# Retention and a wave MLP on one core: the first batch loaded with two tokens per partition in 512-byte rows, and computed by pairs of chunks on 64 by 64 tiles of the array

## The chip, the cores and the metric

The kernel runs on one core of one Trainium2 chip. The metric is the device time in microseconds (us), lower is better. Each run also gives the span from the first to the last instruction and the mean granted clock of TensorE over that span, 1.0 being full speed. A run is called slow here when it is more than 1.5% above the fastest run of the same kernel; ratios use fast runs alone.

## The reference, cut to what matters

```python
# q, k, v: [4 batches, 8 heads, 768 tokens, 64], float32
for t in range(S):                                  # retention, per batch and head
    state = gamma * state + outer(k[t], v[t])
    y[t] = scale * q[t] @ state
x = y with heads side by side                       # [4, 768, 512]
theta = x @ w_theta                                 # 512 x 512
y = w_tok_r @ (x * cos(theta)) + w_tok_i @ (x * sin(theta))   # over tokens, 768 x 768
u = x + y
out = u + relu(u @ w_ch)                            # 512 x 512
```

The kernel cuts the 768 tokens of a batch into six chunks of 128. Within a chunk the recurrence is a masked product of scores (k by q, then by v), and a running state of 64 by 64 a head carries what came before. A token position in a chunk is one of the 128 partitions.

## The kernel before

The loads of the weights and of the first 13 chunks are issued at the start, in an order chosen by hand, on SP's queue; those of the later chunks follow slot by slot. Of q, k and v a chunk is loaded with one token on each partition; a head gives each partition 64 floats, so each row of the transfer is 256 bytes.

```python
def load_chunk(n):
    b, c = divmod(n, nT)
    for name, src in (("kf", k), ("qf", q), ("vf", v)):
        t = io.tile([P, H, D], FT, name=name, bufs=9)
        nc.sync.dma_start(out=t, in_=src[b, :, c*P:(c+1)*P, :].rearrange("h s d -> s h d"))
for what in ("c0 c1 th c2 c3 c4 w0 c5 w1 w2 c6 w3 ch c7 c8 w4 c9 c10 w5 c11 c12").split(): ...
```

"c" is a chunk (three tensors of 256 KB), "th" and "ch" are w_theta and w_ch (1 MB each), "w" a block of 128 rows of each of w_tok_r and w_tok_i (384 KB each; called a pair of w_tok rows below). GpSimd scales and casts a chunk (att_prep), TensorE (PE) transposes k and q (att_T), DVE copies that out (kqT), PE makes the scores (att_A), DVE multiplies by the mask (at), PE makes the products and the state (att_Y), ACT copies the result and the state out, and att_X projects to the angles, of which ACT takes sines and DVE makes z (att_Z). The first batch runs as a software pipeline: chunk n begins while chunk n-1 is finished.

```python
att_prep(0)
for n in range(nT):
    att_T(n)
    if n > 0:
        att_Yinter(n - 1); att_Y(n - 1)
    att_A(n)
    if n > 0: att_X(n - 1)
    if n > 1: att_Z(n - 2)
    ...                                   # w_cast, w_tok, moe_M of the first outputs (cut)
    if n + 1 < nT: att_prep(n + 1)
```

After the first batch a second loop of slots interleaves the attention of chunks 6 to 23 with the products of w_tok by z (moe_M), of u by w_ch (moe_O), and the transposes of w_tok (w_tok). w_ch is cast by GpSimd in slot 0 of that loop.

## Time and profile before

| what | value |
|---|---|
| time, median of the first 3 runs | 184.55 us (183.6 to 186.36) |
| the profiled run | 185.79 us, span 184.0, clock 0.979 |
| PE busy | 161.1 us of 184.0 |
| end of the first batch's part on PE | 42.2 us |
| from there to the end | 141.8 us |

"The first batch's part" ends on PE when three things are done: the third pair of w_tok rows and chunk 6 are transposed, and the products of the first two outputs are complete. I call the time up to that point the head, and the time after it the tail. Two views that the prediction does not show: the stretch from the first to the sixth score group (stretch, length; then busy time and count of PE, PEld, DVE, ACT, POOL; clock, DMA share, GB/s), and from the timeline of PE the end of the head and two later waits (start, duration, engine, line, operation; in brackets the idle time before it and what ended it).

```profile
7.95:31.98 24.03, 19.42 (x207) 12.38 (x208) 14.50 (x19) 12.08 (x23) 15.84 (x17) 1.00 1.18 256
```

### The profile page before, as it was taken

To read this page: it belongs to the slowest core of one execution; us is meant where nothing else is said; L and a number is where in the kernel's file an instruction comes from. 1 tells how busy PE (TensorE), PEld (TensorE's weight loads), DVE (VectorE), ACT (ScalarE), POOL (GpSimd) and SP (SyncE) were. 2 spreads that over 40 slices of the span, in tenths; PEclk is the share of its full clock that TensorE was granted. 3 is DMA by queue.
4 is the path that set the end of the run, shared out by engine and by line. 5 is a ranking of instruction groups with operands and counts; after the bars stand their busy time and mean duration, and the time that the engine had idled before them with its cause. 6 is when DMAs were issued, how large, how long until landed. Compare 5 with 4: busy or idle time off the path is not lost.

```text
span 184.0 us, 3550 instructions
## 1 busy us (share of the span) xinstructions
PE 161.1 (88%) x1392; PEld 91.6 (50%) x1392; DVE 106.1 (58%) x146; ACT 72.6 (39%) x136; POOL 79.9 (43%) x105
## 2 busy tenths in 40 slices
PE   0567997795499989799999999999999999999991
PEld 0244655452265656555655565555545544444560
DVE  1264684736155877868976686756556634534442
ACT  4052754640044645554734544265354342200010
POOL 4648767691977669655859455231000000000000
PEclk9999999999579999999999999999999999999998
DMA  6999999998999989999999999954483333334343
GB/s 133 222 316 218 227 254 279 284 286 242 229 279 218 288 177 222 257 277 231 242 210 254 260 224 188 203 143 114 110 108 100 101 85 77 107 118 114 111 122 116
DMA packets 95265, 35.63 MB, mean 194 GB/s; under 512 B 89488, under 2 KB 89744, under 8 KB 95248
## 3 DMA queue, kind: packets, MB, share of 16 engines
q1 hardware_dynamic: 95104, 35.27, 85.4%
q8 instruction: 11, 0.18, 0.5%
q10 hardware_dynamic: 144, 0.13, 0.2%
q14 instruction: 6, 0.05, 0.1%
HBM read 25.69 MB, written 6.29 MB: 174 GB/s over the span
## 4 chain that ended last, share of the span: by engine, by line
PE 63%; SPq 15%; DMA 9%; DVE 5%; POOL 3%; ACT 1%; issue 1%; DVEq 0%; POOLq 0%
PE y_ps L282 29%; SPq L80 12%; PE o_ps L310 10%; PE th_ps L253 8%; DMA w<-in_moe_w_ch_dram 5%; DMA wtok<-in_moe_w_tok_r_dram 3%; PE at_ps L185 3%; PE yT_ps L214 3%; PE kq_ps L165 3%; SPq L94 2%; PE st_ps L222 2%; DVE at L189 2%; PE x_ps L250 2%; PE yT_ps L203 2%; DMA uT<-u 2%; DVE z L264 1%
## 5 line engine op out<-in xcount | busy, mean ns | idle before, releaser
L282 PE MATMUL y_ps<-z,wtr 128*128 128x512 bf16 x138 | 53.1, 385 | 1.5 <-DVE z L264 1.0
L282 PE MATMUL y_ps<-z,wti 128*128 128x512 bf16 x138 | 53.1, 385 | 0.0
L189 DVE TENSOR_TENSOR at<-at_ps,mask 128x1024 bf16<-128x1024 f32 x24 | 29.3, 1220 | 9.4 <-PE at_ps L185 9.4
L258 ACT ACTIVATE cs<-th_ps,halfpi 128x512 bf16<-128x512 f32 x24 | 16.5, 687 | 38.5 <-PE th_ps L253 38.5
L264 DVE TENSOR_TENSOR z<-cs,x_sb 128x1024 bf16<-128x1024 bf16 x24 | 20.8, 865 | 15.1 <-ACT cs L259 15.0
L154 POOL TENSOR_TENSOR kqb<-qf,qsc 128x512 bf16<-128x512 f32 x24 | 25.2, 1052 | 8.9 <-DMA qf<-in_q_dram 8.7
L156 POOL TENSOR_TENSOR vb<-vf,vsc 128x512 bf16<-128x512 f32 x24 | 25.4, 1060 | 7.5 <-PE yT_ps L214 3.3
L253 PE MATMUL th_ps<-wth,xT 128*128 128x512 bf16 x96 | 25.5, 389 | 1.9 <-DVE wth L393 1.9
L168 DVE COPY kqT<-kq_ps 128x1024 bf16<-128x1024 bf16 x19 | 13.1, 689 | 21.0 <-PE kq_ps L165 21.0
L153 POOL CAST kqb<-kf 128x512 bf16<-128x512 f32 x24 | 16.4, 684 | 18.8 <-DMA kf<-in_k_dram 8.1
L165 PE MATMUL kq_ps<-ident,kqb 128*128 128x128 bf16 x152 | 13.9, 238 | 11.7 <-POOL kqb L153 8.8
L287 DVE TENSOR_TENSOR u<-y_ps,x_sb 128x512 bf16<-128x512 f32 x23 | 15.8, 689 | 13.7 <-PE y_ps L282 13.7
L310 PE MATMUL o_ps<-wch,uT 128*128 128x512 bf16 x92 | 23.5, 380 | 0.1
L231 ACT CAST xT<-yT_ps 128x512 bf16<-128x512 f32 x24 | 14.0, 585 | 24.1 <-PE yT_ps L214 24.0
L313 DVE SCALAR_TENSOR_TENSOR ot<-o_ps,u 128x512 f32<-128x512 f32 x23 | 15.8, 690 | 10.2 <-PE o_ps L310 10.1
L282 PEld LDWEIGHTS <-wti 128*128 128x128 bf16 x138 | 13.6, 99 | 15.5 <-issue 2.6
L282 PEld LDWEIGHTS <-wtr 128*128 128x128 bf16 x138 | 13.6, 99 | 14.1 <-DVE wtr L334 0.7
L165 PEld LDWEIGHTS <-kqb 128*128 128x128 bf16 x152 | 11.0, 106 | 16.8 <-POOL kqb L153 9.2
L259 ACT ACTIVATE cs<-th_ps,zerob 128x512 bf16<-128x512 f32 x24 | 16.3, 680 | 0.0
L236 ACT CAST stbd<-st_ps 64x256 bf16<-64x256 f32 x40 | 14.7, 366 | 0.5
L295 ACT COPY uT<-u_ps 128x512 bf16<-128x512 bf16 x12 | 7.0, 585 | 18.5 <-PE u_ps L293 18.5
L310 PEld LDWEIGHTS <-uT 128*128 128x128 bf16 x92 | 8.7, 98 | 9.8 <-DMA uT<-u 0.3
(51 smaller groups left out, 149.0 us busy)
## 6 DMA issues: line engine op xcount, KB each, us to landing
kf<-in_k_dram SPq DMA_DIRECT2D x24, 256.0 KB, 4.8
qf<-in_q_dram SPq DMA_DIRECT2D x24, 256.0 KB, 5.1
vf<-in_v_dram SPq DMA_DIRECT2D x24, 256.0 KB, 5.3
out_dram<-ot SPq DMA_DIRECT2D x23, 256.0 KB, 2.2
wtok<-in_moe_w_tok_r_dram SPq DMA_DIRECT2D x6, 384.0 KB, 5.3
wtok<-in_moe_w_tok_i_dram SPq DMA_DIRECT2D x6, 384.0 KB, 5.1
w<-in_moe_w_theta_dram SPq DMA_DIRECT2D x1, 1024.0 KB, 6.7
w<-in_moe_w_ch_dram SPq DMA_DIRECT2D x1, 1024.0 KB, 8.5
```

Of the source, the lines that this page charges most:

```text
L80: nc.sync.dma_start(out=t, in_=src[b, :, c * P:(c + 1) * P, :].rearrange("h s d -> s h d"))
L153: nc.gpsimd.tensor_copy(kb.rearrange(r3, h=H), raw[n, "kf"])
L154: nc.gpsimd.tensor_mul(qb.rearrange(r3, h=H), raw[n, "qf"], _bcast_last(qsc[:, c], D))
L156: nc.gpsimd.tensor_mul(vb.rearrange(r3, h=H), raw[n, "vf"], _bcast_last(vsc[:, c], D))
L165: nc.tensor.transpose(kq_ps[:, i * NP + j, :], src[:, j * P:(j + 1) * P], ident)
L189: nc.vector.tensor_mul(at.rearrange("p a j t -> p (a j) t"), at_ps.rearrange("p a j t -> p (a j) t"), _bcast_mid(mask, H))
L253: nc.tensor.matmul(th_ps, s["xT"][:, j, :], wth[:, j, :], start=(j == 0), stop=(j == NP - 1))
L258: nc.scalar.activation(cs[:, 0, :], th_ps, AF.Sin, bias=halfpi, scale=1.0)
L259: nc.scalar.activation(cs[:, 1, :], th_ps, AF.Sin, bias=zerob, scale=1.0)
L264: nc.vector.tensor_mul(zs[b][:, c], st[n]["cs"], _bcast_mid(xs[b][:, c, :], 2))
L282: nc.tensor.matmul(y_ps, wT[r][:, s0, t0 * P:(t0 + 1) * P], zs[b][:, s0, r, :], start=(s0 == 0 and r == 0), stop=(s0 == nT - 1 and r == 1))
L310: nc.tensor.matmul(o_ps, mo[m]["uT"][:, j, :], wch[:, j, :], start=(j == 0), stop=(j == nD - 1))
```

## The change

The intent is to load the first batch in rows twice as long, hoping for a higher DMA rate while the kernel starts. Two neighbouring tokens are adjacent in memory, so a partition that takes both gets 512 bytes in one row. A pair of chunks (256 tokens) is then one tile of 128 partitions by two tokens, and a chunk of 128 tokens is 64 partitions by two. So the scores of a pair become products of 64 by 64, on four tiles of the array. The core of the diff:

```diff
+    def load_pair(g):
+        for name, src in (("k", k), ("q", q), ("v", v)):
+            t = io.tile([P, H, 2 * D], FT, name="pair", bufs=5)
+            nc.sync.dma_start(out=t, in_=src[0, :, 2*g*P:2*(g+1)*P, :].rearrange(
+                "h (p two) d -> p h (two d)", two=2))
...
-    "c0 c1 th c2 c3 c4 w0 c5 w1 w2 c6 w3 ch c7 c8 w4 c9 c10 w5 c11 c12"
+    loads("p0 th p1 w0 p2 w1 w2 c6 w3 c7 ch c8 w4 c9 c10 w5 c11 c12")
...
+    def pair_A(g, two):
+        at_ps = psum.tile([P, 2, NP, P], FT, name="at_ps", tag="at", bufs=1)
+        for j in range(NP):
+            for a in range(2):
+                half = slice(a * HP, (a + 1) * HP)
+                for par in range(2):
+                    rows = slice(par * D, (par + 1) * D)
+                    nc.tensor.matmul(at_ps[half, par, j, :], kT[rows, j, two, half],
+                                     qT[rows, j, :, half], ...)
+        nc.vector.tensor_mul(at..., at_ps..., maskp...)
...
-    for n in range(nT):            # the pipelined loop shown above
+    def pair_in(g):
+        pair_prep(g, "k"); pair_T(g, "k"); pair_prep(g, "q")
+        if g > 0: att_Z(2 * g - 1)
+        pair_T(g, "q"); pair_prep(g, "v")
+        pair_A(g, 0); pair_A(g, 1); pair_Y(g)
+    pair_in(0)
+    att_X(0); att_X(1); att_Z(0)
+    pair_in(1)
+    w_cast(0); att_X(2); w_tok(0); att_X(3); moe_M(0, 0, 2); att_Z(2)
+    pair_in(2)
+    moe_M(0, 2, 4); w_cast(1); att_X(4); w_tok(1); att_X(5); ...
...
-            nc.gpsimd.tensor_copy(wch, wdma["ch"])      # slot 0
+            wch_cast(0, nD)                             # slot 2, four casts on ACT
```

Cut: the second set of decay factors and the mask for pairs, pair_T, pair_Y, fewer buffers for the chunks that are left (7 instead of 9, and 1 instead of 2 for w_theta and w_ch), and the products with w_ch a slot later. In the order of loads chunk 7 also moves ahead of w_ch.

More of the change, by code (lines that the diff above doesn't have):

```diff
@@ L54 @@
     P = 128
+    HP = P // 2
     nT = S // P
@@ L78, in load_chunk @@
         for name, src in (("kf", k), ("qf", q), ("vf", v)):
-            t = io.tile([P, H, D], FT, name=name, bufs=9)
+            t = io.tile([P, H, D], FT, name=name, bufs=7)
             nc.sync.dma_start(
@@ L82, in load_chunk @@
             raw[n, name] = t
+    def load_pair(g):
+        for name, src in (("k", k), ("q", q), ("v", v)):
+            t = io.tile([P, H, 2 * D], FT, name="pair", bufs=5)
+            nc.sync.dma_start(out=t, in_=src[0, :, 2 * g * P:2 * (g + 1) * P, :].rearrange(
+                "h (p two) d -> p h (two d)", two=2))
+            raw[g, name] = t
     wdma = {}
     def load_w512(name, src):
-        t = io.tile([P, nD, dm], FT, name="w512", bufs=2)
+        t = io.tile([P, nD, dm], FT, name="w512", bufs=1)
         nc.sync.dma_start(out=t, in_=src.rearrange("(a p) e -> p a e", p=P))
@@ L95, in load_wtok, with loads @@
         wdma[r, t0] = t
-    for what in ("c0 c1 th c2 c3 c4 w0 c5 w1 w2 c6 w3 ch c7 c8 w4 c9 c10 w5 c11 "
-                 "c12").split():
-        if what == "th":
-            load_w512("th", moe_w_theta)
-        elif what == "ch":
-            load_w512("ch", moe_w_ch)
-        elif what[0] == "c":
-            load_chunk(int(what[1:]))
-        else:
-            for r in range(2):
-                load_wtok(r, int(what[1:]))
+    def loads(order):
+        for what in order.split():
+            if what == "th":
+                load_w512("th", moe_w_theta)
+            elif what == "ch":
+                load_w512("ch", moe_w_ch)
+            elif what[0] == "w":
+                for r in range(2):
+                    load_wtok(r, int(what[1:]))
+            elif what[0] == "p":
+                load_pair(int(what[1:]))
+            else:
+                load_chunk(int(what[1:]))
+    loads("p0 th p1 w0 p2 w1 w2 c6 w3 c7 ch c8 w4 c9 c10 w5 c11 c12")
     posn = const.tile([P, nT], FT)
@@ L127 @@
     nc.scalar.activation(qsc, arg, AF.Exp, bias=lscale, scale=1.0)
+    posp = const.tile([P, nT], FT)
+    nc.gpsimd.iota(posp, pattern=[[2 * P, nT // 2], [1, 2]], base=1,
+                   channel_multiplier=2, allow_small_or_imprecise_dtypes=True)
+    argp = const.tile([P, nT, H], FT)
+    nc.vector.tensor_mul(argp, _bcast_last(posp, H), _bcast_mid(lg, nT))
+    vscp = const.tile([P, nT, H], FT)
+    nc.scalar.activation(vscp, argp, AF.Exp, bias=zerob, scale=-1.0)
+    qscp = const.tile([P, nT, H], FT)
+    nc.scalar.activation(qscp, argp, AF.Exp, bias=lscale, scale=1.0)
     ident = const.tile([P, P], BF)
@@ L133 @@
                             base=0, pattern=[[1, P]], channel_multiplier=-1)
+    maskp = const.tile([P, 2, 2, HP], BF)
+    nc.gpsimd.memset(maskp, 1.0)
+    for a in range(2):
+        for two in range(2):
+            part = maskp[a * HP:(a + 1) * HP, two]
+            nc.gpsimd.affine_select(out=part, in_=part, compare_op=ALU.is_ge, fill=0.0,
+                                    base=-two, pattern=[[1, 2], [2, HP]],
+                                    channel_multiplier=-2)
     stbd = []
@@ L168, in att_T @@
         nc.vector.tensor_copy(kqT, kq_ps)
-        s["kqT"] = kqT
+        s["kT"], s["qT"] = kqT[:, 0:NP, :], kqT[:, NP:2 * NP, :]
     def att_T_dma(n):
@@ L175, in att_T_dma, with pair_prep @@
             out=kqT, in_=s["kqb"].rearrange("p a d -> p (a d)"))
-        s["kqT"] = kqT
+        s["kT"], s["qT"] = kqT[:, 0:NP, :], kqT[:, NP:2 * NP, :]
+    def pair_prep(g, name):
+        t = work.tile([P, 2, dm], BF, name="kqb", bufs=5)
+        src = raw[g, name].rearrange("p h (two d) -> p two h d", two=2)
+        dst = t.rearrange("p two (h d) -> p two h d", h=H)
+        if name == "k":
+            nc.gpsimd.tensor_copy(dst, src)
+        else:
+            for two in range(2):
+                sc = (qscp if name == "q" else vscp)[:, 2 * g + two]
+                nc.gpsimd.tensor_mul(dst[:, two], src[:, two], _bcast_last(sc, D))
+        st[g, name] = t
@@ new lines, in pair_T @@
+    def pair_T(g, name):
+        ps = psum.tile([P, NP, 2, P], BF, name="kq_ps", tag="tr", bufs=2)
+        for two in range(2):
+            for j in range(NP):
+                nc.tensor.transpose(ps[:, j, two, :],
+                                    st[g, name][:, two, j * P:(j + 1) * P], ident)
+        t = work.tile([P, NP, 2, P], BF, name="kqT", bufs=4)
+        nc.vector.tensor_copy(t, ps)
+        st[g, name + "T"] = t
+    def pair_A(g, two):
+        at_ps = psum.tile([P, 2, NP, P], FT, name="at_ps", tag="at", bufs=1)
+        kT, qT = st[g, "kT"], st[g, "qT"]
+        for j in range(NP):
+            for a in range(2):
+                half = slice(a * HP, (a + 1) * HP)
+                for par in range(2):
+                    rows = slice(par * D, (par + 1) * D)
+                    nc.tensor.matmul(at_ps[half, par, j, :], kT[rows, j, two, half],
+                                     qT[rows, j, :, half], start=(j == 0),
+                                     stop=(j == NP - 1), skip_group_check=True)
+        at = work.tile([P, 2, NP, P], BF, name="at", bufs=2)
+        nc.vector.tensor_mul(at.rearrange("p a j t -> p (a j) t"),
+                             at_ps.rearrange("p a j t -> p (a j) t"),
+                             _bcast_mid(maskp[:, two].rearrange("p w i -> p (w i)"), H))
+        st[g, two] = at
@@ new lines, in pair_Y @@
+    def pair_Y(g):
+        yT = [psum.tile([P, NP, P], FT, name="yT_ps", tag="acc", bufs=2)
+              for _ in range(2)]
+        for two in range(2):
+            at, vp = st[g, two], st[g, "v"]
+            for j in range(NP):
+                for a in range(2):
+                    half = slice(a * HP, (a + 1) * HP)
+                    for par in range(2):
+                        h = 2 * j + par
+                        nc.tensor.matmul(yT[a][par * D:(par + 1) * D, j, :],
+                                         vp[half, two, h * D:(h + 1) * D],
+                                         at[half, par, j, :],
+                                         start=(two == 0 and j == 0),
+                                         stop=(g == 0 and a == 0 and two == 1
+                                               and j == NP - 1),
+                                         skip_group_check=True)
+        for a in range(2):
+            c = 2 * g + a
+            half = slice(a * HP, (a + 1) * HP)
+            if c > 0:
+                for j in range(NP):
+                    nc.tensor.matmul(yT[a][:, j, :], stbd[c % 2][:, j, :],
+                                     st[g, "qT"][:, j, :, half], start=False,
+                                     stop=(j == NP - 1), skip_group_check=True)
+            if c < nT - 1:
+                if c == 0:
+                    st_ps[0] = psum.tile([P, NP, P], FT, name="st_ps", tag="st", bufs=1)
+                for two in range(2):
+                    for j in range(NP):
+                        nc.tensor.matmul(st_ps[0][:, j, :],
+                                         st[g, "k"][half, two, j * P:(j + 1) * P],
+                                         st[g, "v"][half, two, j * P:(j + 1) * P],
+                                         start=(c == 0 and two == 0 and j == 0),
+                                         stop=(c == nT - 2 and two == 1 and j == NP - 1),
+                                         skip_group_check=True)
+                state_out(0, c)
+            if c == 0:
+                x_tiles(0)
+            xT = work.tile([P, NP, P], BF, name="xT", bufs=3)
+            nc.scalar.copy(xT.rearrange("e j (i w) -> e j w i", w=2),
+                           yT[a].rearrange("e j (w i) -> e j w i", w=2))
+            st[c] = dict(xT=xT)
@@ L178, in att_A, with state_out, x_tiles @@
+    def state_out(b, c):
+        for par in range(2):
+            sl = slice(par * D, (par + 1) * D)
+            nc.scalar.copy(stbd[(c + 1) % 2][sl, :, sl], st_ps[b][sl, :, sl])
+    def x_tiles(b):
+        xs[b] = big.tile([P, nT, dm], BF, name="x_sb")
+        zs[b] = big.tile([P, nT, 2, dm], BF, name="z")
     def att_A(n):
         s = st[n]
-        kqT = s["kqT"]
         at_ps = psum.tile([P, 2, NP, P], FT, name="at_ps", tag="at", bufs=1)
@@ L184, in att_A @@
                 rows = slice(par * D, (par + 1) * D)
-                nc.tensor.matmul(at_ps[:, par, j, :], kqT[rows, j, :],
-                                 kqT[rows, NP + j, :], start=(j == 0),
+                nc.tensor.matmul(at_ps[:, par, j, :], s["kT"][rows, j, :],
+                                 s["qT"][rows, j, :], start=(j == 0),
                                  stop=(j == NP - 1), skip_group_check=True)
@@ L203, in att_Yinter @@
                 nc.tensor.matmul(s["yT_ps"][:, j, :], stbd[c % 2][:, j, :],
-                                 s["kqT"][:, NP + j, :], start=(j == 0), stop=False,
+                                 s["qT"][:, j, :], start=(j == 0), stop=False,
                                  skip_group_check=True)
@@ L227, in att_Y @@
         if c == 0:
-            xs[b] = big.tile([P, nT, dm], BF, name="x_sb")
-            zs[b] = big.tile([P, nT, 2, dm], BF, name="z")
+            x_tiles(b)
         xT = work.tile([P, NP, P], BF, name="xT", bufs=3)
@@ L233, in att_Y @@
         if c < nT - 1:
-            for par in range(2):
-                sl = slice(par * D, (par + 1) * D)
-                nc.scalar.copy(stbd[(c + 1) % 2][sl, :, sl], st_ps[b][sl, :, sl])
+            state_out(b, c)
     def att_X_dma(n):
@@ L314, in moe_O, with wch_cast @@
         nc.sync.dma_start(out=out[b, t0 * P:(t0 + 1) * P, :], in_=ot)
+    def wch_cast(lo, hi):
+        for a in range(lo, hi):
+            nc.scalar.copy(wch[:, a, :], wdma["ch"][:, a, :])
     wrow = {}
@@ L382, in moe_last @@
                 out=out[b, t0 * P:(t0 + 1) * P, e * hw:(e + 1) * hw], in_=ot)
-    att_prep(0)
-    for n in range(nT):
-        att_T(n)
-        if n > 0:
-            att_Yinter(n - 1)
-            att_Y(n - 1)
-        att_A(n)
-        if n == 1:
-            nc.vector.tensor_copy(wth, wdma["th"])
-        if n > 0:
-            att_X(n - 1)
-        if n > 1:
-            att_Z(n - 2)
-        if n == nT - 2:
-            w_cast(0)
-        if n + 1 < nT:
-            att_prep(n + 1)
-        if n == nT - 2:
-            w_tok(0)
-            moe_M(0, 0, nT - 3)
-        if n == nT - 1:
-            moe_M(0, nT - 3, nT - 2)
+    def pair_in(g):
+        pair_prep(g, "k")
+        pair_T(g, "k")
+        pair_prep(g, "q")
+        if g > 0:
+            att_Z(2 * g - 1)
+        pair_T(g, "q")
+        pair_prep(g, "v")
+        pair_A(g, 0)
+        pair_A(g, 1)
+        pair_Y(g)
+    pair_in(0)
+    nc.vector.tensor_copy(wth, wdma["th"])
+    att_X(0)
+    att_X(1)
+    att_Z(0)
+    pair_in(1)
+    w_cast(0)
+    att_X(2)
+    w_tok(0)
+    att_X(3)
+    moe_M(0, 0, 2)
+    att_Z(2)
+    pair_in(2)
+    moe_M(0, 2, 4)
     w_cast(1)
-    att_Yinter(nT - 1)
-    att_Y(nT - 1)
-    att_Z(nT - 2)
+    att_X(4)
     w_tok(1)
-    moe_M(0, nT - 2, nT - 1)
-    att_X(nT - 1)
+    att_X(5)
     w_cast(2)
     att_prep(nT)
-    moe_M(1, 0, nT - 1)
+    moe_M(1, 0, 4)
+    att_Z(4)
+    moe_M(0, nT - 2, nT - 1)
+    moe_M(1, nT - 2, nT - 1)
+    att_T(nT)
     att_Z(nT - 1)
@@ L420 @@
     moe_M(1, nT - 1, nT)
-    att_T(nT)
     n_of = {i: nT + i for i in range(NCH - nT)}
-    halves, U_at, O_at = {}, {1: 0, 2: 1}, {2: 0, 3: 1}
+    halves, U_at, O_at = {}, {1: 0, 2: 1}, {3: 0, 4: 1}
     for m in range(2, nT):
@@ L476 @@
                 att_X_dma(n_of[s_ - 1])
+        if s_ == 2:
+            wch_cast(0, nD)
         if len(hs) > 1:
```

## The prediction

> **What bounds the kernel now.** I read the page first: busy shares, the 40 slices, the chain of work that ended last. TensorE (PE) is busy 88%, but not evenly, and the DMA rows show why.
>
> ```profile
> span 184.0 us, 3550 instructions
> PE   0567997795499989799999999999999999999991
> PEclk9999999999579999999999999999999999999998
> DMA  6999999998999989999999999954483333334343
> PE 63%; SPq 15%; DMA 9%; DVE 5%; POOL 3%; ACT 1%; issue 1%; DVEq 0%; POOLq 0%
> ```
>
> One digit is 4.6 us. PE is full from about slice 13 (60 us) on; before that it has holes, with the DMA engines at 9. The chain that ended last starts in SP's load queue, passes a transfer of w_ch that lands at 45.4 us, and is then almost only PE. So two regimes: loads set the pace for some 48 us, then matmuls do. Next I asked for busy time by stretches (columns: stretch, its length; busy us and count of PE, PEld, DVE, ACT, POOL; clock, DMA share, GB/s).
>
> ```profile
> 10.00:12.00 2.00, 1.90 (x22) 1.34 (x24) 0.69 (x1) 0.69 (x2) 1.08 (x2) 1.00 1.03 372
> 15.00:19.00 4.00, 4.00 (x30) 2.41 (x29) 0.78 (x2) 1.70 (x3) 2.95 (x5) 1.00 1.38 218
> 30.00:34.00 4.00, 3.64 (x44) 2.19 (x42) 2.27 (x4) 1.52 (x4) 2.66 (x4) 1.00 0.98 342
> 43.90:48.00 4.10, 0.09 (x3) 0.04 (x2) 1.22 (x1) 0.00 (x0) 2.55 (x3) 0.81 0.81 185
> 48.00:53.30 5.30, 4.91 (x32) 2.60 (x34) 1.54 (x3) 0.58 (x1) 4.26 (x5) 0.50 1.03 271
> 54.00:84.00 30.00, 27.80 (x300) 17.46 (x297) 21.78 (x30) 16.15 (x31) 20.36 (x24) 1.00 1.08 238
> 84.00:174.00 90.00, 90.00 (x699) 47.64 (x697) 54.00 (x72) 35.11 (x67) 23.55 (x26) 1.00 0.72 154
> ```
>
> The last column of the first three rows: q, k and v chunks alone (256-byte rows) run at 218 GB/s, the wide rows of w_theta and w_tok at 342 to 372. That is what the change attacks. In 43.9 to 48 PE does nothing, and pays again with the clock at 0.50 until 53.3. From 84 to 174 PE has no idle at all. Last I read the timeline, at the hole and at two undisturbed chunks:
>
> ```profile
> 45.45 1.89 POOL L457 CAST wch<-w 128x2048 bf16<-128x2048 f32 x1 [3.71 <-DMA w<-in_moe_w_ch_dram]
> 47.29 0.61 POOL L153 CAST kqb<-kf 128x512 bf16<-128x512 f32 x1
> 47.96 0.61 PE L165 MATMUL kq_ps<-ident,kqb 128*128 128x128 bf16 x4 [4.01 <-POOL kqb L153]
> ...
> 22.41 0.40 PE L185 MATMUL at_ps<-kqT 64*128 64x128 bf16 x8 [0.42 <-DVE kqT L168]
> 25.67 0.40 PE L185 MATMUL at_ps<-kqT 64*128 64x128 bf16 x8 [0.32 <-DVE kqT L168]
> ```
>
> The hole: GpSimd waits for w_ch, casts it, and only then prepares chunk 7, for which PE waits. The chunks: score matmuls (at_ps) of chunks 3 and 4 are 3.26 us apart. When its data is there, the old software pipeline needs only 3.3 us a chunk.
>
> **What the skill says.** The Trainium skill, "DMA: Bandwidth & Descriptors", Specifications, gives 512 B as the smallest transfer for line rate. The trace agrees in direction (218 against 342 to 372 GB/s); it has no 512-byte row. "TensorE: Matmul & The Clock Gate", Part 1, says the clock is halved after an idle window of about 3.4 us and comes back after a busy one: the trace has 4.0 us idle, then 0.50 for over 5 us. "TensorEngine Tiling (Array Packing)", Tiling Modes, says 64x64 mode gives four tiles that run independently. Eight score matmuls on two row tiles take 0.40 us here; four-wide tiling isn't in this trace.
>
> **The change part by part.**
>
> Loads. Six chunks of three 256 KB tensors, 4.72 MB, take 21.7 us at 218 GB/s. My estimate for 512-byte rows is 283 to 350: a fixed cost per row plus a cost per byte, fitted to 218 at 256 bytes and about 370 at 2 KB, gives 283; the skill's line-rate statement gives about 350. So 16.7 or 13.5 us: 5 to 8 us less DMA work, all early. First pair (512 KB a tensor): bytes start near 2.0 us and the first 256 KB tensor landed at 4.1, so 0.9 us follow the last byte; k lands at 4.4 to 4.8, q at 5.9 to 6.6, v at 7.4 to 8.5.
>
> Compute of a batch-0 pair. This matters more. The instruction order shows no pipelining across pairs: transposes of k, of q, scores A0, scores A1, all products Y, state, both X (projection to angles), then the next pair. at_ps has one buffer, so A1 waits for the mask multiply of A0. Steps with durations from this trace: mask multiply 1.22, kqT copy 0.69, two Sin 1.3 together, z 0.8, xT 0.58, state copies 0.76, th 1.03 with its end. From A0 = 0: scores 0.55 (16 instructions, estimated between 0.40 and 0.6), multiply to 1.8, A1 to 2.4, multiply to 3.7, second half of Y 3.7 to 4.2, state 4.4 to 5.0 (8 matmuls of 64 rows where 4 of 128 took 0.40), state copies on ACT to 5.8, inter matmuls of the second chunk and its state to 6.7, ACT: xT, state copies, xT to 8.1. X of the second chunk ends at 9.4. In the first pair ACT then loads its Sin table (1.28) to 9.4 and does four Sin to 12.0; in the second pair w_tok's copy (0.80) takes that place and Sin ends at 11.5. DVE must do z of the second chunk before it copies the next qT, so 12.0 + 0.8 + 0.7, with waits, gives the next A0 at about 13.8 to 14. Against 2 x 3.3 = 6.6 in the old pipeline.
>
> First A0: q lands 6.6 (slow case), two q multiplies of 1.04 end at 8.7, transposes and copy (second half cold) 1.4, so 10.1. With about 0.8 added for the cold clock in pair 0, A0 of pair 1 is at 24.7, of pair 2 at 38.7. From there to the end of batch 0's part (6.2 of the same chain, then moe products 0.86, X 1.1, w_tok 0.7, X 1.1, a wait for the wti copy 0.5, ten products of w_tok by z 2.1 + 0.5, transposes 0.45, w_tok 0.7, a wait for the last z, four products 0.9) is 15.5 us: 54.2. In the kernel before, the same work (both w_tok(2) and the transposes of chunk 6 done) ended at 42.2. **Cost: 12.0 us**, although the data comes earlier; what remained of the load wait there is already inside 42.2.
>
> What is won back. After 42.2 the old kernel lost 0.3 + 4.0 + 0.4 waiting, and about 2.6 in the half-clock stretch (six 512-wide products at 0.43 instead of 0.215 apart make 1.3, the small groups the rest). w_ch is now cast on ACT (four 128x512 casts, about 0.58 each = 2.3 us, in a stretch, 60 to 66 us, where the same table of stretches had ACT busy 3.2 us of 6) and loaded early enough, so GpSimd isn't blocked: 7.3. Two later waits of x_ps for the wtr copy (0.62 and 1.25) may shrink, I count 0.9; smaller ones 0.5. Chunk 7's preparation still queues behind w_cast(3): -0.7. **Gain: 8.0 us.** Above 84 us nothing changes: PE has no idle there and its instructions are the same.
>
> Sum: span 184.0 + 12.0 - 8.0 = 188.0; the timed median is 0.55 above the profiled span, so 188.5. The chain was added end to end with every step at its full measured duration, and I took the slow load rate, so I put my number 1 us lower: 187.5.
>
> **Rivals.** (1) Load-bound story, the author's: batch 0 is set by transfers, 5 to 8 us fewer of them, and the 4 us hole goes too: 172 to 178. For it: the SP queue heads the chain and DMA sits at 9 in the first 45 us. Against: 3.3 us per chunk is what the old pipeline needs with data present, and the new code drops that pipeline; its chain alone is three times 14 us, longer than the 25 us that loads take. (2) Cold array: with PE busy little over half of each pair cycle the clock could stay at half through batch 0. Matmuls on the path (some 4 us a cycle) would add 2 to 3 us a pair: 193 to 196. For it: PE was half speed until about 19 us in the old kernel also. Against: waits within a pair are near 1 us, shorter than the idle window. (3) 64x64 tiling saves PE time: 48 small instructions a chunk pair more than pay for nothing, since the scores took only 0.40 a chunk; under 1 us either way. (4) The lost time of phase 1 is absorbed: only if PE's later idle exceeded 12 us; measured, it is under 10. That gives 184 to 186 at best.
>
> **Range and chances.** Short steps (13 us cycles, A0 at 9.5, all 9.7 us won back) give a span near 182 to 183; a faster chain than that needs overlap I don't see. Cold clock gives up to 195. The 8-in-10 range is 181 to 194. Below 180.9 (2% faster) batch 0 would have to end before 49 us: 0.13, kept that high because the rest of the schedule was visibly re-tuned around the change. Above 188.2: 0.44. Between: 0.43.
>
> **What would show it.** Score matmul groups of successive pairs 13 to 15 us apart, with PE idle before them for DVE (qT copy, mask multiply) and ACT (stbd, xT); loads of 512 KB running at 280 to 350 GB/s and SP's queue gone from the chain early on; batch 0's part ending near 54 us; no hole at 44 to 48; PE solid afterwards with the same slot lengths. I am wrong if the pair cycle is near 10 us (rival 1), or if PEclk shows halves through batch 0 (rival 2), or if PE has new idle beyond 60 us, which would mean ACT with the wch casts is a bound I took for free.

## More of the kernel before

```profile
41.65 0.61 PE L165 MATMUL kq_ps<-ident,kqb 128*128 128x128 bf16 x8
...
66.58 0.38 PE L250 MATMUL x_ps<-ident,xT 128*128 128x128 bf16 x4 [0.62 <-DVE wtr L334]
77.86 0.38 PE L250 MATMUL x_ps<-ident,xT 128*128 128x128 bf16 x4 [1.25 <-DVE wtr L334]
```

The six score groups took 24.0 us, with PE busy 19.4 of them. The two x_ps waits are on a copy out of w_tok's transposes: x_ps and w_ps share two buffers.

## The result, and the profile after

| | before | after |
|---|---|---|
| time, median | 184.07 us (182.71 to 186.36, 4 runs) | 200.0 us (199.15 to 200.26, 4 runs) |
| profiled span, clock | 184.0, 0.979 | 197.9, 0.951 |
| end of the head | 42.2 us | 61.1 us |
| tail | 141.8 us | 136.8 us |

The ratio is 1.088, with an interval of 1.080 to 1.096: slower by 9%. Ratios here and below are the mean time of one kernel's fast runs over that of the other's of the same rounds, so they are not quite the ratio of the medians quoted.

The page of the changed kernel: span, the slices (4.9 us each here), and the chain that ended last.

```profile
span 197.9 us, 3797 instructions
PE   0448628945998997997999999999999999999990
PEclk9999985596799999999999999999999999999997
DMA  5999995199589999999496886994457445233343
PE 73%; DVE 11%; ACT 6%; DMA 3%; issue 2%; POOL 1%; DVEq 0%; SPq 0%; ACTq 0%; POOLq 0%
```

SP's queue is gone from the chain (15% before, 0% now), and DVE has grown from 5 to 11%. Where the old kernel had one 4 us hole at 44 us, the new one has PE at 2 to 6 tenths several times in the first 50 us, and the clock row has 5s in slices 7 and 8 and a 6 and a 7 in slices 10 and 11. DMA sinks to 1 in slice 8: a transfer waits for a buffer that GpSimd frees only after PE, so the engines that were to be fed better now stand still. Next, the same by stretches, cut at the first score group of each pair (columns as above).

```profile
10.38:26.17 15.79, 9.62 (x116) 6.51 (x116) 7.91 (x9) 6.63 (x11) 10.89 (x11) 1.00 1.15 325
26.17:42.78 16.61, 11.73 (x137) 7.98 (x137) 6.34 (x9) 6.25 (x11) 4.61 (x6) 0.69 0.65 156
42.78:61.10 18.32, 13.63 (x148) 8.29 (x148) 6.89 (x10) 6.21 (x10) 6.87 (x8) 0.81 0.89 208
97.80:188.00 90.20, 90.20 (x698) 47.79 (x696) 53.28 (x73) 34.83 (x67) 18.35 (x21) 1.00 0.63 136
```

A pair of chunks takes 16 to 18 us; PE works 10 to 14 us of it. In the second and third pair the clock is 0.69 and 0.81. The 1.00 of the first pair is not a measurement of full speed: the trace records no change of the clock before about 21.7 us, and until then the same matmuls run at about half speed (four products for the angles took 1.91 us at 18.8 us and 1.03 us at 54.3 us). From 98 to 188 us PE has no idle time, as in the old kernel's 84 to 174. So the loss is in the head. The timeline of PE at the second and third pair:

```profile
26.17 0.42 PE L243 MATMUL at_ps<-kqT 64*64 64x128 bf16 x16 [2.95 <-DVE kqT L231]
27.92 0.42 PE L243 MATMUL at_ps<-kqT 64*64 64x128 bf16 x16 [1.33 <-DVE at L247]
...
42.78 0.42 PE L243 MATMUL at_ps<-kqT 64*64 64x128 bf16 x16 [1.53 <-DVE kqT L231]
44.52 0.42 PE L243 MATMUL at_ps<-kqT 64*64 64x128 bf16 x16 [1.32 <-DVE at L247]
46.26 0.64 PE L262 MATMUL yT_ps<-at,kqb 64*64 64x128 bf16 x16 [1.10 <-DVE at L247]
```

This is a chain without overlap: PE waits for the copy of q's transposes, makes 0.42 us of scores, waits for the mask multiply, makes the other 0.42, waits for the other multiply. The last group takes 0.64 instead of 0.42: the clock has fallen to half. The stretches around that moment:

```profile
43.20:45.20 2.00, 0.64 (x32) 0.49 (x32) 1.44 (x2) 0.00 (x0) 0.00 (x0) 1.00 1.13 270
...
46.20:52.00 5.80, 4.84 (x41) 3.10 (x41) 0.01 (x1) 2.19 (x4) 0.00 (x0) 0.50 1.00 232
```

No single wait here was longer than 1.53 us, yet PE was granted half the clock for the next 6 to 7 us (from about 45.6 to 52.4 us in finer stretches; the earlier one lasts from 28.5 to 38.7). The changes lie on a grid of 3.41 us: 10.2 us and 6.8 us at half clock are three and two steps, and the two falls are five steps apart. Cut on that grid, the trace shows what went before each change:

```profile
21.65:25.07 3.42, 1.57 (x19) 1.18 (x18) 2.43 (x3) 2.11 (x4) 2.18 (x3) 1.00 1.14 340
25.07:28.48 3.41, 0.98 (x48) 0.77 (x48) 2.37 (x4) 0.00 (x0) 3.41 (x4) 1.00 1.10 344
...
35.31:38.72 3.41, 3.40 (x21) 2.26 (x20) 0.83 (x2) 2.61 (x4) 1.43 (x2) 0.50 0.00 0
...
42.13:45.55 3.42, 1.06 (x48) 0.77 (x48) 2.38 (x3) 0.00 (x0) 0.00 (x0) 1.00 1.18 264
```

After the steps in which PE was busy 0.98 and 1.06 us of 3.41 the clock fell; after the one with 1.57 it did not, and after the one with 3.40 it came back.

### The profile page after: what moved, and what is told of

It is laid out like the page before. It is cut to its first block, busy times and chain, and to the rows that moved or that the text cites. A ratio compares the mean times of both kernels' runs of the same rounds, so it can differ in the third digit from the quotient of the medians.

```text
span 197.9 us, 3797 instructions
## 1 busy us (share of the span) xinstructions
PE 166.2 (84%) x1508; PEld 96.4 (49%) x1508; DVE 105.5 (53%) x147; ACT 76.2 (39%) x142; POOL 77.0 (39%) x107
## 4 chain that ended last, share of the span: by engine, by line
PE 73%; DVE 11%; ACT 6%; DMA 3%; issue 2%; POOL 1%; DVEq 0%; SPq 0%; ACTq 0%; POOLq 0%
PE y_ps L405 29%; PE o_ps L433 10%; PE th_ps L376 10%; DVE at L247 4%; DMA pair<-in_q_dram 3%; PE yT_ps L340 3%; PE at_ps L311 3%; PE x_ps L373 2%; PE st_ps L282 2%; DVE z L387 2%; PE kq_ps L198 2%; PE st_ps L348 2%; DVE at L315 2%; ACT stbd L299 2%; PE at_ps L243 2%
## 5 line engine op out<-in xcount | busy, mean ns | idle before, releaser
L376 PE MATMUL th_ps<-wth,xT 128*128 128x512 bf16 x96 | 27.3, 411 | 0.0
L299 ACT CAST stbd<-st_ps 64x256 bf16<-64x256 f32 x40 | 14.6, 366 | 30.3 <-PE st_ps L282 29.9
L315 DVE TENSOR_TENSOR at<-at_ps,mask 128x1024 bf16<-128x1024 f32 x18 | 21.9, 1219 | 5.7 <-PE at_ps L311 5.6
L410 DVE TENSOR_TENSOR u<-y_ps,x_sb 128x512 bf16<-128x512 f32 x23 | 15.8, 690 | 12.1 <-PE y_ps L405 12.0
L189 POOL TENSOR_TENSOR vb<-vf,vsc 128x512 bf16<-128x512 f32 x18 | 19.2, 1065 | 6.1 <-PE yT_ps L340 5.0
L436 DVE SCALAR_TENSOR_TENSOR ot<-o_ps,u 128x512 f32<-128x512 f32 x23 | 15.8, 690 | 9.8 <-PE o_ps L433 9.7
L448 POOL CAST wrow<-wtok 128x768 bf16<-128x768 f32 x12 | 9.8, 823 | 28.7 <-issue 27.2
L187 POOL TENSOR_TENSOR kqb<-qf,qsc 128x512 bf16<-128x512 f32 x18 | 19.6, 1092 | 0.0
L186 POOL CAST kqb<-kf 128x512 bf16<-128x512 f32 x18 | 11.4, 634 | 19.0 <-issue 14.1
L379 DVE COPY x_sb<-x_ps 128x512 bf16<-128x512 bf16 x19 | 7.9, 418 | 18.0 <-PE x_ps L373 18.0
L356 ACT CAST xT<-yT_ps 128x512 bf16<-128x512 f32 x18 | 10.6, 586 | 11.9 <-PE yT_ps L340 11.7
L201 DVE COPY kqT<-kq_ps 128x1024 bf16<-128x1024 bf16 x13 | 9.0, 691 | 9.3 <-PE kq_ps L198 9.3
L376 PEld LDWEIGHTS <-xT 128*128 128x128 bf16 x96 | 9.5, 107 | 8.0 <-issue 2.1
```

Of the source, the lines that this page charges most:

```text
L187: nc.gpsimd.tensor_mul(qb.rearrange(r3, h=H), raw[n, "qf"], _bcast_last(qsc[:, c], D))
L189: nc.gpsimd.tensor_mul(vb.rearrange(r3, h=H), raw[n, "vf"], _bcast_last(vsc[:, c], D))
L299: nc.scalar.copy(stbd[(c + 1) % 2][sl, :, sl], st_ps[b][sl, :, sl])
L315: nc.vector.tensor_mul(at.rearrange("p a j t -> p (a j) t"), at_ps.rearrange("p a j t -> p (a j) t"), _bcast_mid(mask, H))
L376: nc.tensor.matmul(th_ps, s["xT"][:, j, :], wth[:, j, :], start=(j == 0), stop=(j == NP - 1))
L410: nc.vector.tensor_add(u, y_ps, xs[b][:, t0, :])
```

## The experiments

Theories after the result. **Chain and clock:** the unpipelined pair chain costs the 12 us that the prediction worked out, and its sparse PE work lets the clock fall, which costs the rest. **Loads:** the head still waits for data. For the tail, which won back less than predicted: **w_ch** on ACT costs as much as it brings, or **w_tok's** copies hold up what follows. Nine kernels were run; all but the first compute the right result. The number in brackets after a range is the count of runs. The runs of the kernel before vary from job to job (medians 184.47, 183.78, 184.01), so the kernels' own medians and spans are compared, and ratios where they matter.

### 1. Wide rows alone, in the old pipeline (wrong result)

```diff
+    def load_pair(g):                        # as in the change; two chunks out of one tile
+        ...
+            for two in range(2):
+                raw[2 * g + two, name] = t[:, :, two * D:(two + 1) * D]
-    "c0 c1 th c2 c3 c4 w0 c5 w1 w2 c6 w3 ch c7 c8 w4 c9 c10 w5 c11 c12"
+    "p0 th p1 w0 p2 w1 w2 c6 w3 ch c7 c8 w4 c9 c10 w5 c11 c12"
```

Cut: the smaller numbers of load buffers, as in the change. Unlike in the change, w_ch stays ahead of chunk 7. The tokens are in the wrong order, so the output is wrong; every instruction has the old shape. This asks what the longer rows are worth by themselves.

> The kernel before, with only its first batch loaded in 512-byte rows (two tokens per partition; the tokens of a pair come out permuted, so the result is wrong on purpose; order and number of compute instructions are those of before). Theory P (the change lost because the pairs dropped the software pipeline): the wide rows alone help the old pipeline, which is load-bound for its first 40 us: the last score group of batch 0 moves from 32 us to about 27 to 28, and the time falls by 3 to 6 us, to 178 to 181. Rival L (wide rows or their queue order are themselves the harm): no gain or a loss, 184 or more.

Measured: 181.39 us (181.34 to 181.72, 4 runs), clock 0.995 to 1.0 in every run; the kernel before in that job 184.47 (180.96 to 185.97, 7 runs). The ratio of fast runs is 0.9996 (0.994 to 1.005), since it sets aside the old kernel's half-clock runs. The stretch from the first to the sixth score group:

```profile
9.60:33.73 24.13, 18.62 (x203) 12.24 (x207) 15.32 (x19) 11.91 (x23) 18.90 (x21) 1.00 1.00 277
```

The time is near what I expected; the mechanism isn't. The six score groups take 24.1 us, as before (24.0), though the loads moved 277 instead of 256 GB/s meanwhile. And the first group comes 1.65 us later (9.60, before 7.95), because the first data now arrives in pieces twice as large. So faster loads did not shorten the head. They were not without waits, though: between its first and sixth score group GpSimd still waited 4.2 us for pair tensors, each of which lands only as a whole, where it waited 6.6 us for loads in the kernel before; part of what the shorter waits gave was lost in longer steps (one z took 1.33 us instead of 0.68, for instance). What this kernel gains lies at the hole, of which 0.24 + 0.61 us are left: the tail takes 136.1 us (180.0 less 43.9, where its head ends) instead of 141.8. Wide rows, loaded like this, gain a steadier 181.4 us, and no more than the old kernel's own good runs have.

### 2. w_ch cast on ACT in the old kernel

```diff
-            nc.gpsimd.tensor_copy(wch, wdma["ch"])      # slot 0
+        if s_ == 2: wch_cast(0, nD)                     # on ACT
-    O_at = {2: 0, 3: 1}
+    O_at = {3: 0, 4: 1}
```

> The kernel before with only the cast of w_ch moved from GpSimd to ACT (and the first two output products one slot later, as in the change). If the 4 us hole at 44 to 48 us and the half clock after it come from GpSimd waiting for w_ch, as predicted, both go and the time falls by 4 to 7 us, to 177 to 180. If the hole is set by the load of chunk 7 behind w_ch instead, it shrinks by under 2 us and the time stays at 182 to 184.

Measured: 184.43 us (182.52 to 185.46, 4 runs); ratio 1.008 (0.990 to 1.025). Taking the cast off GpSimd did not fill the hole:

```profile
46.03 0.40 PE L165 MATMUL kq_ps<-ident,kqb 128*128 128x128 bf16 x4 [2.05 <-POOL kqb L153]
47.51 0.40 PE L165 MATMUL kq_ps<-ident,kqb 128*128 128x128 bf16 x4 [1.07 <-POOL kqb L154]
```

GpSimd now waits for chunk 7's own transfers, and PE waits 2.05 + 1.07 us for GpSimd (4.01 + 0.40 before). The cast made the hole about 1.3 us longer; it didn't make the hole.

### 3. The changed kernel with PE kept busy

Matmuls of a zero weight tile into the accumulator of the first output, which add zero, are put into the waits of the pair chain. The result stays right, and the chain and all its waits for other engines stay as they are.

```diff
+    def keep_busy(n):
+        for _ in range(n):
+            nc.tensor.matmul(fill["y"], zw, zmov, start=fill.get("first", True), stop=False, ...)
...
         pair_prep(g, "v")
+        keep_busy(1 if g == 0 else 5)
         pair_A(g, 0)
+        keep_busy(3)
         pair_A(g, 1)
         pair_Y(g)                      # with two further groups of 2 inside
```

> The changed kernel with 8 to 12 matmuls by zero weights per pair put into PE's waits (before the scores, between them, before the second half of the products, and after the first state), added to a PSUM bank that is free or where they add zero; the result stays right. Theory C (the part of the loss beyond the predicted 188 is the half clock from 28 to 39 and 46 to 52 us): PE clock stays at 1.00 from about 20 us on, pair cycles fall from 15.8 and 16.6 to about 14 to 14.5, time 193 to 196. Rival (the cycle is set by DVE, ACT and waits alone): cycles within 0.5 us of 16, time 199 to 201.

Measured: 194.0 us (192.56 to 195.6, 4 runs); ratio 1.066 (1.044 to 1.088). The profiled run took 192.69 with a clock of 0.986; the two runs near 195.5 had 0.971 and 0.972. The clock row of the profiled run, the second and third pair, and the tail:

```profile
PEclk9999969999999999999999999999999999999997
```
```profile
24.41 0.42 PE L257 MATMUL at_ps<-kqT 64*64 64x128 bf16 x16 [2.11 <-DVE kqT L235]
...
38.17 0.42 PE L257 MATMUL at_ps<-kqT 64*64 64x128 bf16 x16 [0.46 <-DVE kqT L235]
```
```profile
54.20:191.00 136.80, 127.73 (x1073) 72.08 (x1091) 82.01 (x114) 54.84 (x105) 47.05 (x54) 0.99 0.71 157
```

With work added, the kernel is faster by 6 us in the median and 6.9 in the span. The cycles of the pairs fall from 15.8 and 16.6 to 13.93 and 13.76, and the head ends at 54.2. The tail is 136.8, as in the changed kernel: nothing after the head moved. So the lost clock cost the head the 6 to 7 us. The first pair gains too (15.79 to 13.93), as its matmuls run at full speed from about 14.9 us instead of 21.7. That the end is 54.2 to the tenth, as predicted, is luck; half the runs were some 3 us slower.

### 4. The changed kernel with 256-byte rows

```diff
-            nc.sync.dma_start(out=t, in_=src[0, :, ...].rearrange("h (p two) d -> p h (two d)", two=2))
+            rows = src[0, :, ...].rearrange("h (p two) d -> two p h d", two=2)
+            for two in range(2):
+                nc.sync.dma_start(out=t[:, :, two * D:(two + 1) * D], in_=rows[two])
```

Only the row length of the first batch's transfers is undone; all computing is as in the change.

> The changed kernel with each pair tensor loaded by two transfers of 256-byte rows instead of one of 512-byte rows; everything else, and the result, unchanged. Theory P: the pairs are bound by their own chain, so only the first score group moves, by about 1 us, and the time by 0.5 to 2 us, to 200.5 to 202. Rival L2 (the loads still set batch 0's pace): the 5 us of extra transfer time show in full, 204 to 208.

Measured: 198.05 us (197.86 to 198.24, 4 runs), 1.9 us less than the changed kernel, span 196.2. The same stretch of pure pair loads, in the changed kernel and then in this one:

```profile
5.00:7.00 2.00, 0.83 (x8) 0.77 (x8) 0.00 (x0) 0.00 (x0) 1.14 (x2) 1.00 1.22 290
```
```profile
5.00:7.00 2.00, 0.39 (x4) 0.39 (x5) 0.00 (x0) 0.00 (x0) 1.32 (x2) 1.00 1.35 218
```

The rate does what it should, 290 against 218 GB/s, and the time doesn't rise. The load theory, which had this kernel well above 200 us, is dead. Why it is even faster: 0.85 of the 1.7 us between the two spans lie in the head, and the rest is the last store, which took 1.8 us to land here and 2.7 in the changed kernel's profile; no row length bears on that. In the head, the second pair's scores begin at 25.41 instead of 26.17. In the changed kernel GpSimd's multiply of q ran beside DVE's z at that point; here q's data comes later and z runs alone.

```profile
23.93 2.49 POOL L221 TENSOR_TENSOR kqb<-pair,qscp 128x512 bf16<-128x512 f32 x2 [0.78 <-DMA pair<-in_q_dram]
24.21 1.31 DVE L387 TENSOR_TENSOR z<-cs,x_sb 128x1024 bf16<-128x1024 bf16 x1
```
```profile
24.05 0.70 DVE L389 TENSOR_TENSOR z<-cs,x_sb 128x1024 bf16<-128x1024 bf16 x1
```

The same z took 1.31 us beside the multiply and 0.70 without it, and z stands before the copy of q's transposes on DVE. The Trainium skill, "SBUF — State Buffer", Who interferes with whom, says that a DVE instruction with two inputs in SBUF and a GpSimd instruction that reads SBUF exclude each other; z is of that kind, and the trace agrees: z is 0.61 us longer, where the first of GpSimd's two multiplies still had some 0.75 us to run, and the two multiplies took 2.49 us together instead of the 2.04 of the next two, as if the second had waited for z. Earlier data made an earlier collision.

### 5. The changed kernel with its pairs interleaved again

```diff
-    pair_in(0); att_X(0); att_X(1); att_Z(0); pair_in(1); w_cast(0); att_X(2); w_tok(0); att_X(3) ...
+    pair_start(0, nop, nop)                     # up to the scores; two places for other PE work
+    pair_Y(0)
+    pair_start(1, lambda: att_X(0), lambda: att_X(1))
+    att_Z(0); w_cast(0); w_tok(0)
+    pair_Y(1); att_Z(1)
+    pair_start(2, lambda: att_X(2), lambda: att_X(3))
+    att_Z(2); moe_M(0, 0, 2)
+    pair_Y(2, lambda: moe_M(0, 2, 3)) ...
```

The instructions are the same; only their order changes, so that the projections of one pair stand in the waits of the next pair's transposes and scores.

> The changed kernel with the software pipeline put back between pairs: the projections X of the pair before are placed between the transposes of k and of q and between the two score groups of the next pair, the token-weight transposes and the first moe products fill the wait for the second mask multiply and for the state copy. Same instructions, other order on PE, DVE and ACT; result right. Theory P (the pairs cost because each runs as one chain with nothing between): pair cycles fall from 15.8 and 16.6 to 9 to 11 us, PE stays at full clock, batch 0 ends at 46 to 50 us and the time is 183 to 189. Rival (small 64x64 matmuls or the DVE work of a pair are the bound): cycles stay above 13.5 us, time 192 or more.

Measured: 186.74 us (186.16 to 187.01, 4 runs), clock 0.993 to 1.0; ratio to the kernel before 1.027 (1.019 to 1.035). The second and third pair, and the tail:

```profile
23.30 0.42 PE L243 MATMUL at_ps<-kqT 64*64 64x128 bf16 x16 [0.78 <-DVE kqT L231]
...
32.80 0.42 PE L243 MATMUL at_ps<-kqT 64*64 64x128 bf16 x16 [0.78 <-DVE kqT L231]
```
```profile
48.40:185.20 136.80, 129.00 (x1094) 72.06 (x1091) 82.12 (x114) 54.90 (x105) 47.30 (x54) 0.99 0.74 162
```

The cycles are 12.8 and 9.5 us, the head ends at 48.4 instead of 61.1, the clock holds, and the tail is again 136.8. The order alone carries 13.3 of the 16 us lost (12.7 in the span). What is left against the old kernel is a head that is still 6.2 us longer, of which the tail gives 5.0 back.

### 6. The changed kernel with w_ch cast on GpSimd again

```diff
-        if s_ == 2: wch_cast(0, nD)
+            nc.gpsimd.tensor_copy(wch, wdma["ch"])      # slot 0, as before
```

> The changed kernel with the cast of w_ch back on GpSimd in the first slot after batch 0, as before; nothing else changed. If moving that cast to ACT is worth the removed hole, as predicted, the time rises by 2 us or more, to 202 or more, with PE waiting for chunk 7's preparation. If the hole went because the loads have long arrived when batch 0 ends this late, the cast costs GpSimd 1.9 us that chunk 7 has to wait for at most: 199.5 to 201.5.

Measured: 199.57 us (199.05 to 199.8, 4 runs), span 197.3 against 197.9. So the move of the cast to ACT gains nothing in the changed kernel, which has no hole with either.

### 7. and 8. The old kernel: chunks ahead of w_ch, then w_tok earlier

```diff
 # 7: experiment 2, and
-    "... c6 w3 ch c7 c8 w4 ..."
+    "... c6 w3 c7 c8 ch w4 ..."
 # 8: experiment 7, and in the slot loop
         moe_M(*hs[0])
+        if s_ in (1, 3, 5): w_tok(3 + s_ // 2)          # was after moe_O
```

> The kernel before with the cast of w_ch on ACT (as in the second experiment, which left PE waiting 2.05 + 1.07 us for chunk 7) and chunks 7 and 8 loaded ahead of w_ch. If the hole is chunk 7's transfer queued behind 1 MB of w_ch, the wait for chunk 7 falls under 1 us, PE never goes to half clock and all runs come out near the fast runs of before or below: 178 to 181.5, with no run over 183. If the hole is set by the sum of all bytes loaded, it moves to a later chunk and the time stays at 181 to 185.

> The previous kernel with the three late token-weight transposes (w_tok 3 to 5) moved from the end of their slots to behind the first half of the moe products. The prediction took the waits of x_ps for the wtr copy (0.62 and 1.25 us before, 0.48, 0.89 and 1.31 after the change) as half won back by the change; they were not. If they come from w_ps holding both transpose banks while DVE is behind with mask and output work, they mostly go: 1 to 2.5 us below the previous kernel. If they only move (T or Y waits instead), within 0.5 us of it.

Measured: 7 took 185.19 us (183.08 to 186.34, 6 runs), ratio 1.004 (0.998 to 1.010); 8 took 183.65 us (183.19 to 184.55, 6 runs), ratio 1.000 (0.996 to 1.004). In 7 the wait for chunk 7 is gone (in 8, with the same loads, 1.10 us of it remain), and in its place there is one for chunk 9 ten microseconds later. GpSimd had waited 3.90 us for a pair of w_tok rows, now behind w_ch, and prepared chunk 9 after it:

```profile
56.04 0.40 PE L165 MATMUL kq_ps<-ident,kqb 128*128 128x128 bf16 x4 [2.40 <-POOL kqb L153]
```

A further 1.12 us follow at 57.56. Another order of the same bytes only moves the hole (the profiled run of 7 was slow, but the profiled run of 8, a fast one, has 2.29 + 0.67 us at the same place). With 8 the waits of x_ps for w_tok's copies left x_ps; 0.57 us of such a wait appeared at u_ps. 1.5 us less in the median than 7, and no better than the kernel before.

### 9. The interleaved pairs with w_tok earlier

The edit of 8 on top of experiment 5.

> The interleaved pair kernel with the same move of the token-weight transposes. 1 to 2.5 us below the interleaved kernel's 186.7: 184 to 185.7. To beat the kernel before (fast runs 181 to 182) the pairs would have to win at their start, where the first scores come at 10.5 us against 8.0 and run at half clock; I expect they don't.

Measured: 185.17 us (184.84 to 187.69, 6 runs), ratio 1.007 (1.002 to 1.012), about 1.6 us under experiment 5. Here too the wait moved in part:

```profile
63.02 0.38 PE L418 MATMUL u_ps<-ident,u 128*128 128x128 bf16 x4 [1.73 <-ACT wti L461]
```

It is the best correct form of the change that I ran, and it doesn't beat the kernel before.

## Why the prediction was wrong, point by point

The direction that the sum gave was right (slower, for want of a pipeline), the size was not: 187.5 against 200.0. The gap is accounted for in four terms. The span was predicted as 184.0 + 12.0 - 8.0 = 188.0 and was 197.9.

- **The head, 6.9 us too short: the clock.** This is the step that failed most. The sum took 14 us a pair, the head's end at 54.2, and left the "cold array" to a rival, with the reason that "waits within a pair are near 1 us, shorter than the idle window". The cycles were 15.8, 16.6 and 18.3 us. Against the predicted start of 10.1 and cycles of 14.6, 14.0 and 15.5 that is 0.3 + 1.2 + 2.6 + 2.8 = 6.9. Experiment 3, with the clock mostly held, has 13.93 and 13.76 and ends the head at 54.2. So the chain was worked out rightly, for a clock that the chain itself destroys. The reason given fails because it looks at single waits: none reached 3.4 us (the longest was 2.95), but the clock fell after 3.41 us steps in which PE was busy 0.98 and 1.06 us in all. The rival's size, 2 to 3 us a pair, was right too; it had no weight in the sum. The sign that was named for it, halves in PEclk through the first batch, came. Of the first pair's 1.2 us, about 0.7 is the collision of z with GpSimd's multiply that experiment 4 largely lacks (its cycle is 15.08), which the prediction did not foresee; the remaining 0.5 is not separated from the slow start of PE.
- **What is won back: 5.0 instead of 8.0.** The tail went from 141.8 to 136.8. Cut at the score groups of chunks 6 and 13 (43.55 and 85.69 us before, 63.04 and 99.16 after), the stretch with the hole gained 6.0 us (42.1 to 36.1). The hole's own term, 7.3 less 0.7, fits that: 6.6, less 0.33 by which the two x_ps waits grew, less a new wait of 0.26 for ACT at 75.6. That it fits to the tenth is partly luck: PE does not wait for chunk 7's preparation, for which the 0.7 was taken off; a wait of 0.48 for w_tok's copy stands at 67.66 in its place. From the head's end to chunk 6 the new kernel needs 0.6 more (0.35 of it a wait for DVE's u), and from chunk 13 to the end 0.4 more, which is the last store: after the last instruction of DVE the span goes on for 4.0 us, and for 3.3 before. What failed is the terms for smaller waits, 0.9 and 0.5: the x_ps waits did not shrink.

```profile
79.12 0.38 PE L373 MATMUL x_ps<-ident,xT 128*128 128x128 bf16 x4 [0.89 <-ACT wti L459]
...
91.33 0.38 PE L373 MATMUL x_ps<-ident,xT 128*128 128x128 bf16 x4 [1.31 <-DVE wtr L461]
```

  They are 2.20 us together, where 66.58 and 77.86 of the old timeline have 1.87. The tail's 136.8 with three different heads (61.1, 54.2, 48.4), and 136.1 with the old order and no hole, says that nearly 6 us was all there was to win. Up to DVE's last instruction, without the last store, the tail is 138.5 us before and 132.8 to 132.9 in all four others.
- **From span to time: about 1.6 us.** I added 0.55, the median of the old kernel's times less the span of its profile. But those were different executions: the profiled run took 185.79 for its 184.0, a difference of 1.8. The changed kernel's profiled run took 199.73 for 197.9, and the median is 200.0.
- **The 1.0 us taken off** for steps at full length and the slow load rate had no ground in what the chain did.

Together: 187.5 + 1.0 + 1.55 + 6.9 + 3.0 = 199.95.

Of the readings behind the sum:

- "Loads set the pace for some 48 us" was half wrong. With faster loads the old head keeps its 24 us from first to sixth score group (experiment 1). What faster loads shortened was the hole alone.
- "GpSimd waits for w_ch, casts it, and only then prepares chunk 7" named what the trace shows, but not the cause. Without the cast 3.1 us of waits remain (experiment 2), and with the chunks ahead of w_ch the hole moves (experiment 7): it is the sum of the bytes wanted by that time. In the changed kernel the cast can go back to GpSimd without a hole (experiment 6). That the head now ends 19 us later, so that the loads are ahead, is the likely reason for the closed hole: experiment 4, with 256-byte rows and a late head, has none, and experiment 5, with a head only 6 us longer, hasn't either. Faster loads alone nearly close it too (experiment 1). Part of the cost was thus bound to come back, and no more than the hole's worth.
- The load rate, "283 to 350", was right at its lower end: 290 GB/s at first and about the same elsewhere. The 350 taken from the line-rate statement was not reached.
- First scores at 10.1 were at 10.38. Rival 1 (load-bound) and rival 3 (tiling saves PE time) were rightly turned down: sixteen 64 by 64 matmuls took 0.42 us warm where eight of the old took 0.40, for a pair that has two such groups, as two chunks had. (The count that the prediction gives there is not exact; nothing rests on it.) Rival 4 never arose.
- No hole at the start of the tail and a solid PE after it were predicted, and came: from the head's end on, the waits named in the timeline add up to 3.3 us after (0.35 + 0.48 + 0.26 + 0.89 + 1.31) against 6.6 before (4.01 + 0.40 + 0.33 + 0.62 + 1.25).

When the clock falls can be read off the kept traces. I cut nine of them (before, after, 3 to 9) into steps of 3.41 us on the grid of their own clock changes. All ten falls before a kernel's end came after a step in which PE was busy 0.25 to 0.38 of the time, and the clock stayed up after each of the other 401 steps, which have 0.44 or more. It came back after steps of 0.81 or more, and did not after steps of 0.45 to 0.78 and one of 0.82. Experiment 5, which kept its clock, has no step under 0.61 in its head. This is a pattern in these kernels, with PE's busy time as the profile models it; no run was made to test it.

What stays open: I did not try a pair chain with two score buffers, or z moved off the critical place on DVE.

## What to carry to other kernels

A change of layout that buys bandwidth is paid for in the order of instructions that it breaks: first measure what the transfer is worth with a kernel that moves the same bytes and computes nonsense (here a run as good as the old kernel's best, no more), then count what the lost overlap costs. A chain of dependent steps worked out at full matmul speed is only a lower bound if it leaves PE little to do for a few microseconds (here under 0.4 of a step of 3.41 us), for the clock then falls and lengthens the chain; give this case the centre of the estimate, not the edge. And a hole in front of a late transfer closes by itself when the work before it gets slower, so it must be counted as the cap on what a delay can win back.

## What the Trainium skill lacked or had wrong

- "TensorE: Matmul & The Clock Gate", Part 1, gives as the condition for the half clock at least one idle window of about 3.4 us. Here the clock fell without any such gap: at about 45.6 us, after waits of 1.53 and 1.32 us and in a third of 1.10 us (from 42.13 to 45.55 us PE was busy 1.06 of 3.42), and at 28.5 us, after a wait of 2.95 us and a sparse stretch (0.98 of 3.41). A later section of the same page, "A second HAM failure mode: psum-queue depth-cycling", does say that frequent micro-idles can be enough, but gives no figure. The prediction leaned on Part 1 alone; the two belong together, with numbers like these.
- Part 1 also says that the full clock is back after about 3.4 us of sustained work. Here the half clock lasted 10.2 us (28.5 to 38.7) and 6.8 us (45.6 to 52.4); from 29 to 38 us PE was busy 7.43 of 9 us, and still at 0.50. How busy "sustained" is, the page lacks: in these traces the clock came back after steps of 3.41 us with PE busy 0.81 or more, and stayed down after 0.45 to 0.78 and once 0.82.
- Part 1 notes that the window runs freely and that the slow start varies from run to run, and puts the penalty of that start below 1% of a typical span. For a spread by a half clock in mid-kernel it has no figure: the kernel before took 181.0 to 182.9 us in runs with a clock of 0.995 to 1.0, mostly 183.5 to 186 with 0.985 to 0.99.
- "DMA: Bandwidth & Descriptors", Specifications, gives 512 B as the size for line rate. Rows of 512 bytes ran at 290 GB/s where rows of 256 bytes ran at 218, but the wide rows of the weights at 342 to 372 in the old kernel: better, and not yet the full rate.
